# Spare matmuls in idle slots of TensorE during attention: a schedule change in a four-layer transformer kernel

## The chip, the cores and the metric

The kernel runs on one NeuronCore of one Trainium2 chip. The metric is device time in microseconds (us) of one launch, lower is better. A ratio is the mean time of one kernel's fast runs over that of the other's of the same rounds, so not quite the ratio of the medians that are quoted.

## The reference, cut to what matters

Four residual layers work on x of shape 1 x 2048 x 1024, with 32 heads of 32: two "A" layers with linear attention (feature map of two softmaxes) and two "B" layers with ordinary softmax attention.

```python
x = A_x
x = x + _A_ref(_layernorm(x, axis=-1), A_wqkv, A_w_phi, A_wo)   # layer 0
x = x + _B_ref(_layernorm(x, axis=-1), B_wqkv, B_wo)            # layer 1
x = x + _A_ref(_layernorm(x, axis=-1), A_wqkv, A_w_phi, A_wo)   # layer 2
x = x + _B_ref(_layernorm(x, axis=-1), B_wqkv, B_wo)            # layer 3
# in _B_ref:
scores = jnp.einsum("bhqd,bhkd->bhqk", q, k) * (Dh ** -0.5)
p = _softmax(scores, axis=-1)
o = jnp.einsum("bhqk,bhkd->bhqd", p, v)
```

The exponentials of the two B layers are 2 x 32 x 2048 x 2048 values, all of them ScalarE's work.

## The kernel before

When the Python program is built, it simulates its own engines: it keeps a clock with estimated costs, and each time TensorE's simulated time `st["t"]` advances it decides which instruction comes next. The order that falls out is fixed. TensorE then runs it in that order on the chip, with semaphores for dependences. So the estimated costs stand nowhere in the program and never delay anything on the chip.

Attention is 1024 steps. A step writes scores into two ring buffers in PSUM (there are three), ScalarE turns each buffer (128 x 1024) into exponentials E, and TensorE later multiplies E by V and by ones into a work bank (there are two). Other layers' projections fill TensorE's remaining time where there are any.

```python
MM = 0.216            # the builder's cost of a 512-column matmul group, us
SWITCH = 0.105

def exp_chain(u, kks, e, buf):
    E = yield ("take", e_s)                       # one of nine E buffers
    ...
    yield ("op", "S", c_act(2 * n), lambda x: nc.scalar.activation(
        out=E[:, :, 0:n], in_=ring_t[buf][:, :, 0:n], func=ACT.Exp, scale=INV_SQRT_DH))
    ring.give(buf)
    sums.append((u, kks, e, E))

while True:
    clk.run_until(st["t"])
    ...
    if ready and len(ring.free) >= 2:
        emit_step()          # scores: four row tiles of 32 rows, L1385
        continue
    start_burst()
    if cur_u[0] is not None:
        emit_sum()           # E times V and ones: four column tiles of 32 columns, L1439
        continue
    ...                      # else: a matmul of a projection, an output, a transpose
    if clk.heap:
        st["t"] = max(st["t"], clk.heap[0][0])    # nothing to issue: TensorE idles
        continue
    ...
```

The softmax here doesn't subtract the row's maximum and nothing guards it: scores larger than these inputs give would overflow.

## Time and profile before

| Quantity | Value | View |
|---|---|---|
| Time, median of 3 runs | 2421.17 us | runs |
| Span of the profiled run | 2417.6 us | page |
| ScalarE busy; its exponentials | 2124.7 us; 1910.7 us | page, groups |
| TensorE busy | 2178.1 us (90%) | page |
| Mean granted TensorE clock | 0.912 | cores |

First the page of the kernel before: the span in 40 slices of 60 us. A digit is the busy share in tenths; in the last row it is the clock that TensorE was granted.

```profile
PE   6998999999898799989998999899998887788887
...
ACT  4542699999999999999995489999999999999997
...
PEclk9999999999999699999999999899998576678887
```

ScalarE is at "9" from 300 us on, save where the third layer starts and in the last slice. TensorE's digits fall only to 7 or 8 in the last quarter. But its clock falls to 5 to 8 there, and to 6 in one slice in the middle. Next the windows view, in us busy with the number of instructions in brackets:

```profile
core 0: us, PE busy (x) PEld busy (x) DVE busy (x) ACT busy (x) POOL busy (x), PEclk, DMA share, GB/s
1140.00:1200.00 60.00, 59.79 (x1304) 30.80 (x1300) 38.88 (x59) 59.86 (x70) 8.51 (x12) 1.00 0.29 98
1500.00:1860.00 360.00, 334.80 (x4936) 132.59 (x4924) 176.61 (x341) 352.58 (x391) 53.76 (x68) 0.96 0.49 143
1860.00:2340.00 480.00, 390.74 (x4932) 139.05 (x4932) 183.08 (x276) 454.82 (x489) 70.71 (x64) 0.73 0.23 75
```

The first row is a dense stretch, where projections fill TensorE: full clock, ScalarE idle for 0.14 us of 60. The last row is the thin stretch at the end of layer 3, with little to do for TensorE but scores and sums. The clock is 0.73, and ScalarE, which sets the pace, is idle for 25.2 of 480 us (480 less 454.82). Even so TensorE reads 81% busy there (390.74 of 480), in a stretch where it has too little to do.

The clock's records hold two values only, 1.0 and 0.5, in multiples of 3.413 us; such a step is called a window below. 424 us of the span passed at 0.5, of which 301 us after 1860 us. (The prediction's 425 and 303 count 2 us of the last record past the span's end.)

What that costs is seen in the timeline around 1900 us (start, duration, engine, line, operation, tiles, count; in brackets the idle time before and who ended it):

```profile
1899.34 3.77 ACT L1365 ACTIVATE E<-ring 128x1024 bf16<-128x1024 f32 x4 [0.38 <-PE ring L1385]
...
1900.41 0.61 PE L1385 MATMUL ring<-Q,K2b 32*128 32x512 bf16 x2 [0.74 <-ACT E L1365]
...
1900.95 0.61 PE L1439 MATMUL work<-E,V 128*32 128x512 bf16 x2
...
1901.35 0.64 PE L1439 MATMUL work<-E,V 128*32 128x512 bf16 x2
...
1901.78 0.64 PE L1439 MATMUL work<-E,V 128*32 128x512 bf16 x2
...
1902.20 0.64 PE L1439 MATMUL work<-E,V 128*32 128x512 bf16 x2
...
1902.78 0.61 PE L1385 MATMUL ring<-Q,K2a 32*128 32x512 bf16 x2
...
1903.18 0.64 PE L1385 MATMUL ring<-Q,K2a 32*128 32x512 bf16 x2
1903.48 1.94 ACT L1365 ACTIVATE E<-ring 128x1024 bf16<-128x1024 f32 x2 [0.38 <-PE ring L1385]
```

A group of four sums takes 0.42 us from start to start; where the record reads 1.0, it takes 0.216 us in the same trace (start times of the L1439 matmuls, the commonest value; 0.427 us where it reads 0.5). The scores of 1902.78 stand behind four such groups. ScalarE runs four exponentials, then sits idle for 0.38 us, and again. Four exponentials recur every 4.14 us (1899.34 to 1903.48). Back to back they start every 0.904 us, 3.62 us for four. (One exponential lasts 1.06 us, which is 3.77 us less three times 0.904. Back to back it overlaps the one before by some 0.16 us; after a wait, such as the 0.38 us shown, it does not, so the loss of 0.52 us is more than the idle time shown.) Lastly the groups on which this rests (busy us, mean ns, then the idle time before them):

```profile
L1365 ACT ACTIVATE E<-ring 128x1024 bf16<-128x1024 f32 x2048 | 1910.7, 1124 | 54.1 <-PE ring L1385 48.5
...
L1385 PE MATMUL ring<-Q,K2b 32*128 32x512 bf16 (+1 forms) x2560 | 438.4, 369 | 123.2 <-ACT E L1365 118.1
```

### The profile page before, as it was taken

How to read it: one execution, taken by the hardware profiler on the slowest of the kernel's cores; microseconds unless marked ns; L12 is line 12 of the kernel's file. 1: busy time of each engine (PE TensorE's matmuls, PEld its weight loads, DVE VectorE, ACT ScalarE, POOL GpSimd, SP SyncE). 2: the span in 40 equal slices, each digit the busy share in tenths (PEclk: the TensorE clock that was granted, in tenths of full speed). 3: DMA queues.
4: the chain of work that ended last, by engine and by line, in shares of the span. 5: the costliest groups of instructions: out<-in, count | busy, mean ns of one | idle time of the engine just before them, and what ended most of it. 6: DMA issues, size and time to landing. Idle time of an engine off the chain costs nothing.

```text
span 2417.6 us, 70484 instructions
## 1 busy us (share of the span) xinstructions
PE 2178.1 (90%) x30290; PEld 937.9 (39%) x30334; DVE 1306.8 (54%) x2341; ACT 2124.7 (88%) x2482; POOL 407.3 (17%) x500
## 2 busy tenths in 40 slices
PE   6998999999898799989998999899998887788887
PEld 4554444344343133435554543333333121224343
DVE  6877444545545376887658754545435155232522
ACT  4542699999999999999995489999999999999997
POOL 4212101111102122231123200201102022110200
PEclk9999999999999699999999999899998576678887
DMA  6652665654434244333235465453634432111100
GB/s 219 178 190 78 179 206 178 195 180 141 136 128 141 70 126 157 96 91 103 103 113 193 140 194 173 135 167 109 167 132 154 162 101 79 32 56 39 56 28 21
DMA packets 213801, 311.08 MB, mean 129 GB/s; under 512 B 91504, under 2 KB 109936, under 8 KB 210672
## 3 DMA queue, kind: packets, MB, share of 16 engines
q1 hardware_dynamic: 186768, 196.47, 27.0%
q0 software_dynamic: 26720, 110.11, 13.7%
q8 instruction: 237, 3.88, 0.7%
q14 instruction: 76, 0.62, 0.1%
HBM read 203.23 MB, written 84.41 MB: 119 GB/s over the span
## 4 chain that ended last, share of the span: by engine, by line
PE 74%; ACT 15%; issue 5%; DVE 4%; DMA 1%; POOL 0%; SPq 0%; ACTq 0%; another core or an unknown queue 0%; DVEq 0%; POOLq 0%
PE work L452 24%; PE work L1439 20%; PE ring L1385 16%; ACT E L1365 13%; PE work L455 9%; PE ring L455 3%; DVE blk L438 2%; ACT blk L763 1%; PE work L838 1%; DMA kvacc<-blk 1%; PE work L993 0%; DVE sm L804 0%; DMA slab<-in_A_wqkv_dram 0%; PE ring L838 0%; DVE blk L1233 0%
## 5 line engine op out<-in xcount | busy, mean ns | idle before, releaser
L1365 ACT ACTIVATE E<-ring 128x1024 bf16<-128x1024 f32 x2048 | 1910.7, 1124 | 54.1 <-PE ring L1385 48.5
L1439 PE MATMUL work<-E,V 128*32 128x512 bf16 (+1 forms) x5120 | 641.5, 387 | 7.0 <-DVE blk L438 4.4
L1439 PE MATMUL work<-E,ones 128*32 128x512 bf16 (+1 forms) x5120 | 641.4, 387 | 0.0
L1385 PE MATMUL ring<-Q,K2b 32*128 32x512 bf16 (+1 forms) x2560 | 438.4, 369 | 123.2 <-ACT E L1365 118.1
L1385 PE MATMUL ring<-Q,K2a 32*128 32x512 bf16 (+1 forms) x2560 | 441.5, 371 | 48.5 <-ACT E L1365 48.4
L438 DVE TENSOR_TENSOR blk<-blk,work 128x512 f32<-128x512 f32 (+1 forms) x289 | 196.0, 680 | 413.8 <-PE work L1439 352.6
L1439 PEld LDWEIGHTS <-V 128*32 128x32 bf16 x5120 | 253.4, 106 | 235.3 <-issue 155.7
L438 POOL TENSOR_TENSOR blk<-blk,blk 64x512 bf16<-64x512 f32 (+1 forms) x156 | 167.9, 1077 | 783.3 <-DVE blk L1233 682.7
L1385 PEld LDWEIGHTS <-K2a 32*128 32x128 bf16 x2560 | 122.0, 93 | 444.7 <-issue 438.3
L1197 DVE COPY blk<-work 128x512 f32<-128x512 f32 (+1 forms) x160 | 93.4, 584 | 361.4 <-PE work L1439 359.4
L1439 PEld LDWEIGHTS <-ones 128*32 128x32 bf16 x5120 | 249.5, 106 | 32.2 <-issue 2.4
L1385 PEld LDWEIGHTS <-K2b 32*128 32x128 bf16 x2560 | 144.9, 93 | 224.3 <-issue 217.6
L1233 DVE RECIPROCAL blk<-blk 128x128 f32<-128x128 f32 x252 | 224.9, 925 | 2.1
L452 PE MATMUL work<-slab,blk 128*32 128x512 bf16 x2768 | 180.2, 382 | 1.0 <-DVE blk L438 0.9
L452 PE MATMUL work<-slab,xnT 128*32 128x512 bf16 (+1 forms) x2208 | 134.2, 368 | 2.5 <-DVE blk L438 1.2
L452 PE MATMUL work<-xnT,slab 128*32 128x512 bf16 x2048 | 136.0, 385 | 0.1
L455 PE MATMUL work<-slab,xnT 128*128 128x512 bf16 (+1 forms) x524 | 115.4, 372 | 2.6 <-DMA slab<-in_A_wqkv_dram 1.7
L763 ACT ACTIVATE blk<-work 128x512 bf16<-128x512 f32 x88 | 48.1, 595 | 76.2 <-PE work L455 70.1
L455 PEld LDWEIGHTS <-xnT 128*128 128x128 bf16 x808 | 79.0, 99 | 83.7 <-issue 7.7
L452 PEld LDWEIGHTS <-blk 128*32 128x32 bf16 x3176 | 73.6, 96 | 87.5 <-issue 34.2
L438 POOL TENSOR_TENSOR blk<-blk 128x256 bf16<-128x256 f32 x95 | 68.4, 731 | 200.6 <-DVE blk L438 166.4
L452 PEld LDWEIGHTS <-slab 128*32 128x32 bf16 x2816 | 66.1, 96 | 77.8 <-issue 29.9
(173 smaller groups left out, 2219.8 us busy)
## 6 DMA issues: line engine op xcount, KB each, us to landing
pd<-blk SPq DMA_DIRECT2D x146, 256.0 KB, 2.5
blk<-pd SPq DMA_DIRECT2D x146, 256.0 KB, 3.3
slab<-in_B_wqkv_dram POOLq DMA_DIRECT2D x32, 1024.0 KB, 6.4
Q<-qd SPq DMA_DIRECT2D x121, 256.0 KB, 2.8
qd<-blk SPq DMA_DIRECT2D x64, 256.0 KB, 2.2
x<-blk SPq DMA_DIRECT2D x48, 256.0 KB, 2.9
blk<-x SPq DMA_DIRECT2D x48, 256.0 KB, 4.0
blk<-in_A_x_dram SPq DMA_DIRECT2D x32, 256.0 KB, 3.9
```

The source lines that it names most:

```text
L438: return ("op", e, cost, lambda x: eng(x).tensor_tensor(out=o, in0=a, in1=b, op=op))
L452: nc.tensor.matmul(o[js], lhsT=l[:, js], rhs=r, start=st, stop=sp, tile_position=(0, 32 * j), skip_group_check=True)
L455: nc.tensor.matmul(o, lhsT=l, rhs=r, start=st, stop=sp, skip_group_check=True)
L763: yield ("op", "S", c_act(C), lambda x, s=s: nc.scalar.activation(out=e[:, s * C:(s + 1) * C], in_=src, func=ACT.Exp, scale=1.0 - 2.0 * s))
L838: nc.tensor.matmul(bank[:, 129 * j:129 * (j + 1)], lhsT=e[:, s * C + gl * P:s * C + (gl + 1) * P], rhs=va_b[l, tg, h][:, gl, :], start=(j ...
L1197: yield ("op", "V", c_ps(n), lambda e: nc.vector.tensor_copy(out=a, in_=bank[:, 0:n]))
L1233: yield ("op", "V", 0.06 + 0.0063 * P, lambda e, x=x: nc.vector.reciprocal(out=r[:, x:x + P], in_=r[:, x:x + P]))
L1365: yield ("op", "S", c_act(2 * n), lambda x: nc.scalar.activation(out=E[:, :, 0:n], in_=ring_t[buf][:, :, 0:n], func=ACT.Exp, scale=INV_SQR ...
L1385: nc.tensor.matmul(ring_t[bufs[e]][:, j, i * n:(i + 1) * n], lhsT=K2[e][c][u.g // 4][r, u.g % 4, m, :], rhs=u.Q[r, e, 0:n], start=True, st ...
L1439: nc.tensor.matmul(u.acc[r0 + 32 * j:r0 + 32 * j + 32, 0:n], lhsT=lh, rhs=E[:, j, i * n:(i + 1) * n], start=u.first, stop=end, tile_positi ...
```

## The change

Its intent is to keep TensorE's clock up in thin attention phases. Where the builder finds nothing to issue, and its own record of the last 3.4 us holds less than 70% of matmul time, it issues one group of four matmuls into a PSUM bank that no one is using. The results are never read.

```diff
+    PSC = sorted(sg[2] for sg in STAGES if sg[0] == "PS")
...
-            clk.start(xslot(u, 17 if l == 0 else 24))
-            if l == 0:
+            beside = l == 2 and c in PSC
+            clk.start(xslot(u, 24 if beside else 17))
+            if not beside:
                 clk.start(spill(u))
... (three more lines of the same kind, for other lists of stages)
+    recent = []
+    idb = ident[:].unsqueeze(1).to_broadcast([P, 4, P])
... (emit_step, emit_sum and the filler append their time and cost to recent)
         if clk.heap:
+            if work and st["t"] - st["last"] < 3.0 and clk.heap[0][0] - st["t"] > 0.1 and st["ui"] < len(units):
+                while recent and recent[0][0] < st["t"] - HAM:
+                    recent.pop(0)
+                if sum(x[1] for x in recent) < WARM * HAM:
+                    set_mode("col")
+                    for j in range(4):
+                        nc.tensor.matmul(work[-1][32 * j:32 * (j + 1), :], lhsT=ones[:], rhs=idb, start=True, stop=True,
+                                         tile_position=(0, 32 * j), skip_group_check=True)
+                    st["t"] += MM
+                    recent.append((st["t"], MM))
+                    continue
             st["t"] = max(st["t"], clk.heap[0][0])
             continue
...
+HAM = 3.4
+WARM = 0.7
```

## The prediction

> **What bounds the kernel now.** From about 300 us on, ScalarE's softmax exponentials set the pace: 2048 of them, 1910.7 us of ScalarE's 2124.7 busy us (page, groups and busy table). Back to back they start every 0.904 us (timeline). In the dense stretch 1140 to 1200 us ScalarE idles 0.1 us (windows). In the last one, 1860 to 2400 us, TensorE has little other work, ScalarE is idle for 29 us, and the granted clock is 0.57 to 0.85 (clock row: 5 to 8).
>
> The clock records read only 1.0 or 0.5, in steps of 3.413 us.[...] 425 us are spent at 0.5, 303 us of them after 1860 us and 48 us between 770 and 860. I worked out array activity per window from matmul shapes and start times. At full clock, windows under 0.35 are nearly always followed by the half clock, those over 0.45 never. At half clock, 0.85 of that clock always brought the full one back. TensorE still reads 76 to 86% busy there.
>
> At half clock a group of four column-tiled matmuls takes 0.427 us (timeline) against 0.23 us at full clock (chain: 32 matmuls in 1.84 us). Scores then queue behind value sums, and ScalarE loses about 0.54 us on every fourth exponential: four take 4.15 us at 1900 us instead of 3.62. After 1860 us, exponentials starting at half clock exceed the 0.904 us pitch by 43 us in all; at full clock by 2 us. Between 770 and 860 us it is 7.5 us; in 1500 to 1860 about 7 us.
>
> **What the change does.** The spill and loader edits do nothing: all four PS stages are listed. Only spare matmuls count: 859 groups of four (3436 matmuls, as many weight loads) into a free work bank, placed by the builder's clock where the last 3.4 us hold under 0.7 of matmul time. By position against this trace about 600 fall after 1860 us, 90 in 780 to 840, 58 in 1680 to 1860, none before 600 us. Estimate: 859 x 0.23 = 198 us of TensorE time.
>
> Activity of 0.7 lies far above what keeps the clock, so it should stay near 1.0 there. The price: a score group may wait behind a spare (up to 0.2 us, as with filler in dense stretches, which lose only 13 to 16 ns per exponential); and 129 spares wait on a VectorE semaphore, since the bank taken is the one freed last.
>
> **Sum.** Nearly all is on the critical path. Tail: 45 us of lost pitch to about 8: -37. 770 to 860: -6. Other thin spots: -5. New waits behind spares and VectorE: +4. About -44 us: 2377 us, 1.8% faster. Range 2362 to 2400. Faster by over 2%: 0.37; within: 0.60; slower: 0.03.
>
> **What would show it.** Right: mean clock from 0.912 to about 0.98, after 1860 us above 0.95; ScalarE idle there 29 to under 10 us; stretches before 600 us unchanged. Wrong: clock still low (spares don't count as activity, or are too few in real time); clock high but ScalarE idle before exponentials (spares delay scores); spares waiting long on VectorE.
>
> **What would make it wrong.** The builder's clock drifting from the chip's; bank waits stalling the in-order matmul queue; freed time lost to query loads or VectorE.

-37, -6, -5 and +4 make -44 us. Shares of activity per window are estimates, worked out from the matmul shapes, start times and clock records of the trace of the kernel before.

## More of the kernel before

Different sets of runs came from different chips, and the kernel before is re-timed beside each set; its median was 2421 to 2427 us. For that reason ratios are compared across sets, not times.

## The result, and the profile after

| | before | after |
|---|---|---|
| median of 4 runs | 2422.92 us | 2388.76 us (2382.76 to 2392.26) |
| ratio | 1 | 0.9861, 95% interval 0.9832 to 0.9890 |
| profiled span | 2417.6 us | 2381.0 us |
| mean granted clock of the profiled run | 0.912 | 0.992 |

The result is correct against the reference. The same rows of the page, after:

```profile
PE   6998999999999999998999899999999999999998
...
ACT  4542689999999999998996479999999999999997
...
PEclk9999999999999999999999999899999999999999
```

The clock is at "9" in all slices but one, and in the last quarter TensorE reads 9 up to the last slice but one. The windows, in the same order as before:

```profile
1140.00:1200.00 60.00, 59.78 (x1321) 32.12 (x1314) 37.56 (x58) 59.86 (x72) 7.68 (x11) 1.00 0.32 108
1500.00:1860.00 360.00, 339.03 (x5056) 134.15 (x5056) 170.67 (x337) 343.11 (x380) 52.59 (x67) 0.97 0.48 140
1860.00:2340.00 480.00, 458.10 (x7652) 188.84 (x7644) 189.55 (x288) 479.99 (x524) 73.88 (x68) 1.00 0.24 77
```

In the thin stretch ScalarE is idle for 0.01 us where it was 25.2. The middle row tells of the opposite: between 1500 and 1860 us ScalarE is now idle for 16.9 us (360 less 343.11) where it was 7.4. The timeline near the same place as before:

```profile
1897.02 8.78 ACT L1369 ACTIVATE E<-ring 128x1024 bf16<-128x1024 f32 x9
...
1899.43 0.39 PE L1389 MATMUL ring<-Q,K2b 32*128 32x512 bf16 x2
...
1899.76 1.26 PE L1560 MATMUL work<-ident,ones 128*32 128x512 bf16 x20
...
1900.95 0.39 PE L1389 MATMUL ring<-Q,K2a 32*128 32x512 bf16 x2
...
1901.59 0.40 PE L1560 MATMUL work<-ident,ones 128*32 128x512 bf16 x4
...
1901.82 0.38 PE L1444 MATMUL work<-E,V 128*32 128x512 bf16 x2
...
1902.03 0.38 PE L1444 MATMUL work<-E,V 128*32 128x512 bf16 x2
...
1903.42 0.83 PE L1560 MATMUL work<-ident,ones 128*32 128x512 bf16 x12
```

The exponentials run without idle time (nine in a row in this view), the scores are ready before they are needed, and a group of sums takes 0.21 us, half of the 0.42 us in the timeline before. The groups:

```profile
L1369 ACT ACTIVATE E<-ring 128x1024 bf16<-128x1024 f32 x2048 | 1900.3, 1223 | 31.1 <-PE ring L1389 21.4
...
L1389 PE MATMUL ring<-Q,K2b 32*128 32x512 bf16 (+1 forms) x2560 | 401.9, 338 | 54.2 <-ACT E L1369 43.0
...
L1560 PE MATMUL work<-ident,ones 128*32 128x512 bf16 x3436 | 240.1, 382 | 1.8 <-DVE blk L438 0.6
```

TensorE idled for 1.8 us in all before the spares, 0.6 us of it ended by the VectorE operation named most, although 129 of them carry a wait for VectorE.

Lining up the two traces by the number of the exponential shows where the time went. This table is worked out from start times of the exponentials (us from the first to the last of the stretch; positive is a loss):

| exponentials | before | after | difference |
|---|---|---|---|
| 512 to 576 (776 to 840 us before) | 64.4 | 58.5 | -5.9 |
| 832 to 896 (1090 to 1153 us) | 63.2 | 70.3 | +7.1 |
| 1152 to 1472 (1527 to 1837 us) | 309.7 | 320.7 | +11.0 |
| 1472 to 2047 (1837 to 2404 us) | 566.5 | 527.1 | -39.4 |
| all others, and the ends | | | -9.4 |
| span | 2417.6 | 2381.0 | -36.6 |

So the gain in the tail is there in full, and 18 us are given back in two places. The first is this, in the timeline after:

```profile
1101.42 0.28 PE L1444 MATMUL work<-E,V 128*32 128x256 bf16 x2
...
1101.99 2.08 ACT L1369 ACTIVATE E<-ring 128x1024 bf16<-128x1024 f32 x2
...
1107.45 0.40 PE L1444 MATMUL work<-E,ones 128*32 128x256 bf16 x2 [5.75 <-issue]
...
1110.24 1.02 ACT L1369 ACTIVATE E<-ring 128x1024 bf16<-128x1024 f32 x1 [6.17 <-PE ring L1389]
```

TensorE stops for 5.75 us in the middle of a burst of sums and waits for no semaphore ("issue"); ScalarE then idles for 6.17 us until the next scores. The trace's DMA records show two instruction fetches in flight at that time, 16 KB in 5.31 us from 1098.6 us and 8 KB in 4.40 us from 1103.03 us; the median of all fetches is 0.96 us. The second ended at 1107.43 us, TensorE went on at 1107.45. A slab of 1 MB and a DMA transpose were under way beside them. (Whether the fetches were the cause stays open; see "What stays open" below.) The second place shows in the waits between 1500 and 1860 us (total us, times, longest), before and after:

```profile
ACT E L1365 <- PE ring L1385: 4.4, 9, 1.3
...
ACT E L1365 <- PE work L1439: 2.5, 3, 1.3
...
PE work L452 <- DMA kvacc<-blk: 0.4, 1, 0.4
```

```profile
ACT E L1369 <- PE ring L1389: 9.0, 6, 3.3
...
ACT E L1369 <- PE work L1444: 7.8, 9, 1.5
...
PE work L452 <- DMA kvacc<-blk: 3.0, 1, 3.0
PE work L452 <- DMA slab<-in_B_wqkv_dram: 2.7, 1, 2.7
```

ScalarE waits more for TensorE, both for scores ("ring") and for an E buffer that the sums still hold ("work"), and TensorE stands for 3.0 and 2.7 us in front of a DMA that it hardly waited for before.

### The profile page after: what moved, and what is told of

It is laid out like the page before. It is cut to its first block, busy times and chain, and to the rows that moved or that the text cites. A ratio compares the mean times of both kernels' runs of the same rounds, so it can differ in the third digit from the quotient of the medians.

```text
span 2381.0 us, 77399 instructions
## 1 busy us (share of the span) xinstructions
PE 2249.9 (94%) x33770; PEld 994.2 (42%) x33770; DVE 1303.7 (55%) x2341; ACT 2113.8 (89%) x2482; POOL 407.0 (17%) x500
## 4 chain that ended last, share of the span: by engine, by line
PE 72%; ACT 15%; issue 6%; DVE 4%; DMA 2%; POOL 0%; SPq 0%; ACTq 0%; DVEq 0%; POOLq 0%
PE work L452 24%; PE work L1444 15%; PE ring L1389 15%; ACT E L1369 13%; PE work L455 9%; PE work L1560 4%; PE ring L455 3%; DVE blk L438 2%; ACT blk L764 1%; PE work L840 1%; DMA kvacc<-blk 1%; DMA slab<-in_A_wqkv_dram 0%; DMA slab<-in_B_wqkv_dram 0%; DVE sm L806 0%; PE ring L840 0%
## 5 line engine op out<-in xcount | busy, mean ns | idle before, releaser
L1444 PE MATMUL work<-E,ones 128*32 128x512 bf16 (+1 forms) x5120 | 543.7, 340 | 5.8 <-issue 5.8
L1444 PE MATMUL work<-E,V 128*32 128x512 bf16 (+1 forms) x5120 | 543.6, 340 | 5.3 <-DVE blk L438 3.2
L1389 PE MATMUL ring<-Q,K2b 32*128 32x512 bf16 (+1 forms) x2560 | 401.9, 338 | 54.2 <-ACT E L1369 43.0
L1389 PE MATMUL ring<-Q,K2a 32*128 32x512 bf16 (+1 forms) x2560 | 416.8, 342 | 2.5 <-ACT E L1369 2.4
L1444 PEld LDWEIGHTS <-V 128*32 128x32 bf16 x5120 | 237.6, 97 | 155.3 <-issue 71.0
L1389 PEld LDWEIGHTS <-K2a 32*128 32x128 bf16 x2560 | 112.7, 91 | 388.5 <-issue 382.8
L1444 PEld LDWEIGHTS <-ones 128*32 128x32 bf16 x5120 | 233.7, 97 | 48.2 <-issue 6.3
L1560 PE MATMUL work<-ident,ones 128*32 128x512 bf16 x3436 | 240.1, 382 | 1.8 <-DVE blk L438 0.6
L1389 PEld LDWEIGHTS <-K2b 32*128 32x128 bf16 x2560 | 151.4, 91 | 148.7 <-issue 142.3
L1560 PEld LDWEIGHTS <-ones 128*32 128x32 bf16 x3436 | 76.4, 95 | 101.2 <-issue 56.0
```

Source lines behind the costliest of these rows:

```text
L1389: nc.tensor.matmul(ring_t[bufs[e]][:, j, i * n:(i + 1) * n], lhsT=K2[e][c][u.g // 4][r, u.g % 4, m, :], rhs=u.Q[r, e, 0:n], start=True, st ...
L1444: nc.tensor.matmul(u.acc[r0 + 32 * j:r0 + 32 * j + 32, 0:n], lhsT=lh, rhs=E[:, j, i * n:(i + 1) * n], start=u.first, stop=end, tile_positi ...
L1560: nc.tensor.matmul(work[-1][32 * j:32 * (j + 1), :], lhsT=ones[:], rhs=idb, start=True, stop=True, tile_position=(0, 32 * j), skip_group_c ...
```

## The experiments

Theory 1: the gain is the clock, held up by the spares' activity; the loss between exponentials 1152 and 1472 comes from the new order of the other instructions, because spares move the builder's clock. Rivals: (2) the gain comes from the new order; (3) the loss comes from the time that the spares take on TensorE; (4) the number of instructions matters. That order did change was checked in the built programs: both kernels have 30334 matmuls besides the spares, their orders first differ near the 6975th, and most between exponentials 1152 and 1472.

One part needed no chip: the kernel with the whole change except the spares builds to the same order on all five engines as the kernel before. So the edits of spill and loader do nothing here.

All twelve runs gave correct results; each time is the median of 4 runs. "Ratio" is to the kernel before, of the same rounds.

| run | time us | ratio (95% interval) | clock of profiled run |
|---|---|---|---|
| 1 again | 2383.45 | 0.9840 (0.9819 to 0.9862) | 0.989 |
| 2 phantom | 2431.34 | 1.0035 (1.0017 to 1.0053) | 0.910 |
| 3 keep | 2370.11 | 0.9785 (0.9768 to 0.9801) | 0.992 |
| 4 one | 2379.32 | 0.9826 (0.9799 to 0.9854) | 0.989 |
| 5 keep_one | 2376.76 | 0.9803 (0.9788 to 0.9819) | 0.990 |
| 6 keep_50 | 2380.84 | 0.9812 (0.9791 to 0.9832) | 0.982 |
| 7 keep_35 | 2406.01 | 0.9924 (0.9906 to 0.9942) | 0.947 |
| 8 keep_tiny | 2472.86 | 1.0201 (1.0155 to 1.0248) | 0.922 |
| 9 keep_again | 2376.17 | 0.9790 (0.9762 to 0.9819) | 0.991 |
| 10 keep_tail | 2389.95 | 0.9846 (0.9823 to 0.9869) | 0.972 |
| 11 keep_60 | 2375.54 | 0.9786 (0.9767 to 0.9805) | 0.986 |
| 12 keep_quarter | 2373.85 | 0.9781 (0.9759 to 0.9804) | 0.989 |

The number before a run's name is that of its section below. The first four ran on one chip, the next four on a second, the last four on a third.

### 1. The change again

No edit.

> The changed kernel again, unchanged. Its earlier runs gave 2383 to 2392 us, so 2380 to 2393 us is expected, mean clock 0.985 to 0.992. What is open is the 5.75 us idle gap of TensorE at 1101.7 us of its trace, where no semaphore was awaited and an instruction fetch of 16 KB took 5.3 us. If it is a chance meeting with a large transfer, it is absent or elsewhere here; if it belongs to the changed instruction stream, it is at the same place again. The two PE waits on DMA at 1590 us (2.95 us) and 1723 us (2.7 us) should recur if they come from the order of instructions.

The stall of TensorE near exponential 862 was absent: exponentials 832 to 896 took 63.1 us, as before. The waits on the two DMAs were there again (2.2 us at 1590 us, 2.5 us at 1723 us), and exponentials 1152 to 1472 took 317.5 us against 309.7 before. So that part is not chance, while the stall does not come every time with this instruction stream.

### 2. The order of the change without its spares

```diff
                     set_mode("col")
-                    for j in range(4):
-                        nc.tensor.matmul(work[-1][32 * j:32 * (j + 1), :], lhsT=ones[:], rhs=idb, ...)
                     st["t"] += MM
```

> All decisions of the changed kernel's builder, so its order of all other instructions, but no spare matmul is issued. Theory 1 (the gain is the clock that the spares hold up, the loss is the new order): the clock falls back to about 0.91, the tail is slow again, and the order's loss of some 5 to 19 us stays: 2423 to 2440 us, slower than the kernel before. Theory 2 (the gain comes from the new order): about 2389 us with the clock still low.

It came out 9 us slower than before, with the clock down to 0.910: theory 1's side. The last stretch and the waits of 1500 to 1860 us:

```profile
1860.00:2340.00 480.00, 392.99 (x4890) 138.10 (x4888) 182.84 (x275) 452.97 (x487) 69.21 (x62) 0.73 0.23 75
```

```profile
ACT E L1369 <- PE work L1444: 7.6, 8, 1.5
...
ACT E L1369 <- PE ring L1389: 5.1, 8, 1.6
...
PE work L452 <- DMA slab<-in_B_wqkv_dram: 2.5, 1, 2.5
...
PE work L452 <- DMA kvacc<-blk: 1.6, 1, 1.6
```

The clock of 0.73 and ScalarE's idle time of the kernel before are back (27 of 480 us), so the new order gains nothing in the tail. The wait for the E buffers (7.6 us against 7.8) and the wait on the slab's DMA (2.5 us) are those of the change, though not one spare was issued. Exponentials 1152 to 1472 took 316.3 us: the order alone loses 6.6 us in this trace, where the change lost 11.0 in its first trace and 7.8 in its repeat. Rival 2 falls, and rival 3 falls for that part.

### 3. Spares without a say in the order

```diff
-            if work and st["t"] - st["last"] < 3.0 and clk.heap[0][0] - st["t"] > 0.1 and st["ui"] < len(units):
-                (as in the change)
+            if work and st["t"] - st["last"] < 3.0 and st["ui"] < len(units):
+                t = st["t"]
+                while clk.heap[0][0] - t > 0.1:
+                    while recent and recent[0][0] < t - HAM:
+                        recent.pop(0)
+                    if sum(x[1] for x in recent) >= WARM * HAM:
+                        break
+                    (the four spare matmuls)
+                    t += MM
+                    recent.append((t, MM))
             st["t"] = max(st["t"], clk.heap[0][0])
```

A local time `t` places the spares in the gap; `st["t"]` then goes on as if there had been none. The built program has 887 groups of spares, and all else in exactly the order of the kernel before.

> Spares as in the change (887 groups of four), but the builder's clock does not count them, so all other instructions on TensorE stand in exactly the order of the kernel before. Theory 1 (the loss at exponentials 1152 to 1472 comes from the new order): that loss of 10 to 12 us goes, the tail keeps its gain of 39 us: 2365 to 2378 us. Rival (the spares' own time on TensorE makes the loss): the loss stays or grows, 2385 to 2395 us.

2370.11 us: 0.9785 against 0.9840 for the change on the same chip. The tail kept its gain (exponentials 1472 to 2047: 528.0 us against 566.5), and 1152 to 1472 took 306.3 us, 3.4 us less than before where the change took 320.7. Its waits between 1500 and 1860 us:

```profile
ACT E L1369 <- PE work L1444: 2.2, 2, 1.3
...
ACT E L1369 <- PE ring L1389: 1.4, 4, 0.6
```

From 7.8 and 9.0 us to 2.2 and 1.4, with as many spares between exponentials 1152 and 1472 as in the change (160 matmuls in either trace). Rival 3 is refuted: the spares' own time does not make the loss. This version beats both kernels.

### 4. One full matmul for each spare

```diff
-                    for j in range(4):
-                        nc.tensor.matmul(work[-1][32 * j:32 * (j + 1), :], lhsT=ones[:], rhs=idb, ..., tile_position=(0, 32 * j))
+                    nc.tensor.matmul(work[-1][:], lhsT=ident[:], rhs=idb, start=True, stop=True, skip_group_check=True)
```

> Each spare is one full 128x128 matmul of 512 columns in place of four column tiles of 32: same array work and time, 859 instead of 3436 matmuls, other instructions in the order of the change. If only the activity counts, the clock stays at 0.98 to 0.99 and the time within 0.5% of the change, 2378 to 2392 us. If the longer instruction stream costs fetch stalls, it is 5 us or more faster than the change. If switching between tiled and full mode costs time, it is slower and ScalarE idles more in the tail.

0.9826 against 0.9840 for the change: no difference within the intervals, at a quarter of the spare instructions. The clock is the same, 0.989 as in experiment 1 and 1.00 from 1870 to 2340 us, with spares whose operands are an identity matrix and copies of it, mostly zeros. That such a spare takes the same time shows in experiment 5's trace, where it lasts 382 ns on average, as each of the change's four does. So a cost of the number of instructions (rival 4) does not show beyond the noise; whether the 4 us between the medians are real stays undecided. In its trace exponentials 1152 to 1472 took 313.0 us, a loss of 3.3 us, the smallest of the four traces with the new order.

### 5. Both of these

Experiment 3 with the spare of experiment 4.

> Order of the kernel before, and each spare one full 128x128 matmul in place of four column tiles (887 in place of 3548 matmuls). If the order's loss and the shape of a spare are independent: within 0.3% of the order-kept run, 2363 to 2376 us, clock 0.985 or more. If mixing full-array matmuls between tiled ones costs ScalarE time: 5 us or more slower than it.

2376.76 us, just outside the range, ratio 0.9803 against 0.9785, with overlapping intervals on two chips: inconclusive for the small difference. In the profiled run a part of it is a stall like the first trace's: TensorE idle for 3.7 us at 1108 us without a semaphore to wait for. So few spare instructions do not rule that stall out.

### 6 and 7. Lower targets

`WARM = 0.5` (406 groups) and `WARM = 0.35` (218 groups) in experiment 3's kernel.

> Order kept, target activity 0.5 in place of 0.7: 406 groups of four in place of 887. Theory (the clock falls only after a window under about 0.4 and the rest of the spares buy nothing): clock 0.97 or more, 2368 to 2380 us. If 0.7 is needed to hold the clock: clock about 0.94, 2390 to 2405 us.

> Order kept, target 0.35: 218 groups of four, which lies below the activity that kept the clock in the trace of before (0.45 and over: never lost; under 0.35: lost in 56 of 58 windows). Theory: the clock falls in most of the tail's windows, 0.92 to 0.95, and most of the gain is lost: 2395 to 2418 us. If any activity, however thin, holds the clock (a matter of gaps, not of the sum): clock 0.98 and about 2370 us.

At 0.5 the time was 2380.84 us, a little over its range. The clock was lost in a few of the tail's windows (it reads 0.98 from 1870 to 2340 us), and this trace also had a wait of 3.6 us on a DMA transpose at 664 us, which comes and goes from run to run (0.65 us in the kernel before, 3.3 to 4.5 us in three later traces, one of them without any spare so early). At 0.35 most of the gain is gone, 2406.01 us. Its last stretch:

```profile
1860.00:2340.00 480.00, 404.70 (x5548) 146.33 (x5549) 186.28 (x281) 461.78 (x499) 72.13 (x66) 0.82 0.23 75
```

In the kernel before, with windows of 3.41 us and an activity worked out from the trace's matmul shapes and start times (an estimate; each matmul counts whole in the window in which it starts), the tail's windows at full clock that lost it had at most 0.38 of the array in use, those that kept it at least 0.38. From 300 to 2350 us the losing ones reached 0.425 by this estimate; with each matmul's time split at the window's borders they had at most 0.379, in the traces before and after, and those that kept it at least 0.367. Long gaps do not explain it: in the kernel before the clock stayed at half for up to 37.5 us on end, while no gap of TensorE between 1860 and 2400 us was over 1.02 us. So the amount counts in these traces, and a margin was needed: from 1870 to 2340 us the clock reads 0.81 at the target 0.35, 0.98 at 0.5 and 1.00 at 0.7. The builder's 3.4 us are counted by its own clock, not by the chip's.

### 8 and 12. Spares of a sixteenth and of a quarter of the array

```diff
+                    # experiment 8: 32 rows x 32 columns
+                    nc.tensor.matmul(work[-1][0:32, :], lhsT=ones[0:32, :], rhs=idb[0:32], ..., tile_position=(0, 0))
+                    # experiment 12: 128 rows x 32 columns
+                    nc.tensor.matmul(work[-1][0:32, :], lhsT=ones[:], rhs=idb, ..., tile_position=(0, 0))
```

Each in place of the four matmuls, in experiment 3's kernel, and counted by the builder as before. (In its trace the sixteenth lasts 443 ns on average, at a mean clock of 0.922; a spare of the change lasts 382 ns, at 0.992. With the quarter TensorE is busy for 457.92 of the last 480 us, with the full spares of experiment 3 for 458.57.) "The monitor" in the two expectations stands for whatever sets the granted clock; what that is, no run here shows.

> Order kept, same times and number of spares as the order-kept run, but each is one 32x32 tile of 512 columns, a sixteenth of the array, as long in time. If the monitor counts busy time of TensorE: clock 0.985 or more and 2365 to 2378 us. If it counts the share of the array in use (activity then about 0.38 in the tail): clock 0.92 to 0.95 and 2395 to 2420 us.

> Order kept, same times and number of spares as at 0.7, each one column tile of 32 over all 128 rows, a quarter of the array. If the monitor weighs the share of the array in use, activity in the tail is about 0.44 at full clock, at the edge of what kept the clock: 0.95 to 0.985, 2375 to 2410 us, between the full spares (2370 us) and the sixteenth (2473 us). If anything above a tile counts as full, 2370 us and 0.99.

The last stretch of the two, the sixteenth first:

```profile
1860.00:2340.00 480.00, 469.95 (x4818) 157.22 (x4811) 178.69 (x268) 427.21 (x456) 67.22 (x59) 0.81 0.24 79
```

```profile
1860.00:2340.00 480.00, 457.92 (x6029) 188.62 (x6027) 188.65 (x289) 479.78 (x524) 72.76 (x68) 1.00 0.23 73
```

The sixteenth was off its range on the bad side, 2472.86 us: TensorE reads 98% busy (469.95 of 480) and yet the clock is 0.81. So busy time alone does not keep the clock. These spares don't hold the clock and do harm: ScalarE is idle for 53 of 480 us, and over the whole run 90.8 of the 116.0 us idle before exponentials ended when scores came (54.1 us, 48.5 of them until scores came, in the kernel before). That each takes some 0.42 us at half clock, as a group of sums does in the kernel before, and that the scores wait behind it, is my estimate of the cause. The quarter did as well as the full spares, clock 1.00 in the tail, 0.989 in all and ratio 0.9781, where the share of the array was expected to give 0.95 to 0.985 and 2375 to 2410 us. So my expectation, the share of the array, is wrong as well. From the full spare to the quarter only the columns changed, and the clock held (1.00 and 1.00 in the tail); from the quarter to the sixteenth only the rows changed, and it did not (0.81). That the share of the rows in use decides, whatever the columns, is no more than my estimate from these three clocks: a spare of 32 rows and 128 columns, which would try it, was not run.

### 9. Experiment 3 again

> The order-kept kernel again, beside the three others on one chip: 2366 to 2376 us, ratio to before 0.976 to 0.981. If the stall of 4 to 6 us near exponential 862 (TensorE idle[...] in 4 of 8 traces with spares) is a matter of chance, this trace may show it although the first of this kernel did not.

0.9790 against 0.9785 in the first set: it repeats, though the time of 2376.17 us is 0.2 us over its range. The stall near exponential 862 is absent here; the wait on the DMA transpose at 659 us was 4.5 us this time.

### 10. Spares in the tail alone

```diff
-            if work and st["t"] - st["last"] < 3.0 and st["ui"] < len(units):
+            if work and st["t"] - st["last"] < 3.0 and st["ui"] < len(units) and nstep[0] >= 745:
```

`nstep` counts the score steps.

> Order kept, spares only from step 745 of 1024 (exponential 1490) on: 646 of the 887 groups. Theory: the tail's gain of 39 to 40 us is there whole, the 8 to 12 us of the earlier thin stretches are gone: 2378 to 2387 us, 9 to 14 us above the order-kept kernel. Up to exponential 1472 the trace is that of the kernel before, and no TensorE stall near exponential 862, if that needs spares before it. Rival (the early spares move what comes later, too): the tail gains less than 35 us.

The time missed the stated range by 3 us, on a chip whose kernel before ran 5 us above the first. Measured in the trace, exponentials 1472 to 2047 took 529.1 us, 37.4 less than before (38.5 with all spares, experiment 3): the tail's gain without any earlier spare (2 us short of what theory 1 said, above the rival's 35). The ratio is 0.9846 against 0.9790 for all spares on that chip, so the earlier thin stretches are worth about 14 us (0.0056 of 2427) with intervals as wide as that; I had counted 11 us for them.

### 11. Target 0.6

> Order kept, target 0.6: 606 groups. Between the targets 0.5 (2381 us, some windows of the tail still cold) and 0.7 (2370 us): 2368 to 2380 us, clock 0.985 or more, no cold window in the tail. If each spare had a cost of its own, this would beat 0.7 by 2 us or more.

2375.54 us, ratio 0.9786 against 0.9790 for 0.7: the same, with a third fewer spares (606 groups against 887); a few windows of the tail were at half clock all the same (0.99 from 1870 to 2340 us). A full spare in an idle slot has no cost that these runs can see.

## Why the prediction was right

The measured 2388.76 us lies in the range 2362 to 2400, "within 2%" was the likeliest class, and 34 us of the forecast 44 us came. Point by point:

- The mechanism. "Only spare matmuls count" is right: the built program without them is the old one. That the clock is the cause is shown by the phantom run (same order, no spares, clock 0.910, no gain).
- Clock. Predicted 0.98 and over 0.95 in the tail; measured 0.985 to 0.992 in the change's four runs and 1.00 in the tail.
- Tail: predicted -37 us, measured -39.4. ScalarE's idle time there "29 to under 10 us": 0.01 us of 480.
- 770 to 860 us: predicted -6, measured -5.9 (exponentials 512 to 576).
- Other thin spots: predicted -5. The table's last line has -9.4 for the profiled run, but the same stretches of its repeat (experiment 1) come to -0.5, so this term is not shown and most of the 9.4 is chance. In 420 to 480 us there are no spares, and the 2.1 us that the first trace gained there are absent in the repeat; exponentials 960 to 1024 gained 2.7 us in the first trace and lost 1.7 in the repeat.
- "New waits behind spares and VectorE: +4" is the term that was mis-sized, and its cause was misplaced. The losses in the profiled run are 18.1 us, in its repeat 7.8. Waits before spares came to 1.8 us, and scores were hardly held up (0.01 us of idle ScalarE in the tail). What the prediction had listed only among its risks, the builder's clock drifting, happened in another way. Spares advance the builder's clock, the order of all later instructions shifts, and in the crowded stretch of 1500 to 1860 us the new order makes ScalarE wait for E buffers and TensorE for a DMA: 6.6 us with the order alone, 3.3 to 11.0 us with the spares added (experiments 1 and 4 and the change), -3.4 us with the old order and spares. The remaining 7.1 us are a stall that a run has or hasn't. That the total still fell inside the range owes something to the range, which reached 23 us above the forecast of 2377.

What stays open: which single decision of the builder makes the new order worse, and why its loss varied from 3.3 to 11.0 us among the four traces that have it. The stall near exponential 862 was seen in six of the eleven traces that have spares before that place (5.75 us in the change, 3.7 in keep_one, 5.2 in keep_35, 4.2 in keep_tiny, 2.3 in keep_60, 0.8 in keep_quarter) and in none of the three that have not (before, phantom, keep_tail). With three such traces that is no proof that spares bring it on. Nor is a slow fetch shown to be its cause. In two of the six traces (the change and keep_35) a 16 KB fetch took 5.3 and 3.9 us at that time; in the other four no fetch near the stall took over 1.5 us. The cause of the stall stays open.

## What to carry to other kernels

Where another engine sets the pace and TensorE looks 80% busy, read the granted clock: here it was 0.73 in a stretch where TensorE had too little to do and read 81% busy, and cheap matmuls into a free bank brought it to 1.00 and won back the pace of the other engine (ScalarE's idle time there went from 25.2 to 0.01 us). Count such filler out of whatever decides the order of the real work, or its gain is partly lost to an order that nobody chose (here 52 us of gain against 34 to 39). Filler must be strong enough to hold the clock: here a target of 0.6 was enough (clock 0.986, ratio 0.9786), 0.35 lost most of the gain (0.947, 0.9924), and filler on a corner of the array made the kernel slower than none (0.922, 1.0201).
